# A delta-rule attention and two MoE layers on one core: the first part's order as an explicit list, and the key products in 64x32 tiles

## The chip, the cores and the metric

One core of a Trainium2 chip runs the whole program. The metric is the device time in microseconds (us) of one execution, where lower is better. It is told as the median of several runs.

## The reference

Three layers run one after the other on 4 batches of 768 tokens, 3072 tokens in all, 384 wide.

1. A delta rule with 8 heads of 48. With k normalized, each head keeps a 48x48 state. At every token `y_t = q_t S`, and then `S += beta_t * k_t (v_t - k_t S)`. The tokens of one sequence depend on each other in order.
2. A dense feed-forward layer with 2048 inner columns: `h = x w_in`, `g = h * clip(h + 3, 0, 6) / 6`, `x = g w_out`.
3. A mixture of 8 experts: each token goes to the expert with the largest gate, through `relu(x w1) w2`, weighted by its probability.

All inputs and outputs are float32, and the kernel keeps that accuracy by splitting each operand into a high and a low half and by adding three products (high by high, high by low, low by high).

## The kernel before, in words

**Chunks.** The delta rule is done in 12 chunks of 64 tokens. Two batches lie beside each other on the 128 partitions, so there are 24 iterations `it`: chunk `it // 2`, batch pair `it % 2`. Four iterations make a group `g`, and there are six groups.

**The first part** (up to about 506 us of the span) holds the delta rule and the first 7 of the 16 slices of 128 inner columns of the dense layer. It is written as 31 Python generators, called streams. Each yields one operation at a time, or a list of TensorE products that stay together. The ones that matter here:

- `kl_stream`, `n_stream`, `k_stream`: load k, take its norms (tiles `ksq`, `ss`, `s`, `rn`), and write the normalized k as a high and a low half into `Kbd`. `kt_stream` and `kg_stream` turn it by DMA transposes into `KTb`, `QTb` or `KG`.
- `g_stream` (line 603): the key products `pG`, for each iteration the products of all keys of a chunk with each other. Each of the 8 heads takes 3 products for each of the two 64-partition halves, so 48 products. From them ScalarE copies the diagonal 32x32 blocks into `Dt` (four copies of 32 partitions) and writes the off-diagonal block as two halves `MC`.
- `t_stream` (line 634), `s_stream`, `z_stream`: for each group a VectorE transposition `Bt<-Dt`, a product with beta on GpSimd, a substitution of 31 steps of two VectorE operations (`sub`, `Xp`), a transposition `Bt<-Xp`, the halves `TT`, and the products `pZ` of 32x32 tiles.
- `chain(0)`, `chain(1)`: the recurrence of each batch pair, with products `pR`, `pW` twice and `pS`, each 24 products, and evictions by ScalarE and VectorE between them. `o_stream` makes the output products `pO` (96 products of 64x64 tiles); `p_stream` makes `pP`, `x_stream` the transposes `pX`.
- `m_stream`: the dense layer of a chunk, 84 rounds in all of 9 products `ph`, the activation (ScalarE `t`, VectorE `t`, ScalarE `gH`, GpSimd `gL`) and 6 products `py`. `wi_stream` and `wo_stream` prepare its weights; four VectorE operations on `nws` narrow each slice.
- `ahead_stream`: the first three slices of the weights for the second part.

**What sets the order.** `drive` (line 1078) runs the streams while the program is built. `Clock` (line 39) holds a planner's costs of each operation; `drive` takes the operation that could start first by these costs and breaks near ties by the table of due times `DUE`. `pin` (line 164) then ties each operation to the one before it on its engine, so each engine's order is fixed in the program. On the chip an engine takes its operations in that order, each as soon as its inputs are there. The loads and the DMA transposes are issued by SyncE, also in the order in which they were planned.

**The second part** is the rest of the dense layer (lines 1410 to 1480), then the routing and the experts. No line of it is touched.

Of the kernel before, what the change touches and what calls it, by code (L numbers as in the profile page):

```python
# [38 lines left out]
class Clock:  # L39


    def __init__(self, tc):
        self.tc, self.last = tc, {}
        self.free = dict(pe=0.0, act=0.0, dve=600.0, pool=3100.0, dma=0.0)
        self.columns = {}
        self.written, self.read, self.bus, self.issue = {}, {}, 0.0, 0.0
        self.slot, self.count, self.parts = {}, {}, {}
        self.runs, self.phase, self.tick, self.warm = [], 0.0, 0, False
        self.mode = 128, False
        self.place, self.end = {}, dict(act=0.0, dve=0.0)  # L50

    def tile(self, pool, shape, dt, tag, bufs, name):
        t = pool.tile(shape, dt, tag=tag, name=name, bufs=bufs)
        n = self.count[tag] = self.count.get(tag, -1) + 1
        self.slot[t.name] = (tag, n % bufs)
        return t

    def keys(self, ap):

        n = ap.name  # L60
        if n in self.parts:
            return [(n, x) for x in self.parts[n](ap)]
        return [self.slot.get(n, n)]

    def cost(self, op):

        n = 1
        for d in (op.ins[0] if "reduce" in op.fn.__name__ else op.out).shape[1:]:
            n *= d
        if "dma" in op.fn.__name__:  # L70
            return 40
        half = (op.ins[-1] if op.eng == "pe" else op.out).dtype in (FP16, FP32R, BF16)
        if op.eng == "pe":
            if op.ins[-1].dtype == FP32R:
                return n / 2.2
            if op.ins[-1].shape[0] <= 64:
                return max(32 if op.ins[-1].shape[0] == 64 else 25.2, n / 2.4) / op.tiles
            return max(25.5, n / 2.4 + 2.5) if half else 0.85 * max(n, 128)
        fn = op.fn.__name__
        pointers = sum(x.free_size() == 1 for x in op.ins[1:])  # L80
        if op.eng == "act":
            return (52 if op.ins[0].space == PSUM else 109) + 95 * (pointers > 0) + 84 * (len(op.outs) > 1) + 0.836 * n
        if op.eng == "dve":
            if half and fn == "tensor_copy":
                return 64 + 0.26 * n
            if fn == "memset":
                return 60 + (0.38 if half else 0.82) * n
            if fn == "transpose":
                return 70 + 1.06 * n
            if fn == "reciprocal":  # L90
                return 70 + 6 * n
            if fn == "tensor_scalar" and op.ins[0].space != PSUM:
                return 66 + 0.52 * n + 60 * (pointers > 0)
            return 70 + (0.52 if all(x.dtype == FP16 for x in op.ins) else 1.04) * n + 60 * (pointers > 0)
        if op.eng == "pool":
            if fn in ("memset", "tensor_copy"):
                return 80 + 0.81 * n
            wide = op.out.dtype == FP32R or op.out.shape[-1] == 32
            return 60 + (2.5 if wide else 2.15) * n
        raise ValueError(op.eng)  # L100

    def places(self, op):

        r, w = {}, (op.out.space, op.out.start_partition())
        for x in op.ins:
            r.setdefault(x.space, x.start_partition())
        return r, w

    def held(self, op):

        r, w = self.places(op)
        now = self.place.setdefault(op.eng, ({}, {}))
        return any(now[0].get(m, x) != x for m, x in r.items()) or now[1].get(w[0], w[1]) != w[1]

    def shared(self, op):

        if op.eng != "dve" or op.fn.__name__ in ("memset", "transpose", "tensor_reduce", "reciprocal"):
            return False
        wide = [x for x in op.ins if x.free_size() > 1]
        sb = [x for x in wide if x.space != PSUM]  # L120
        if op.fn.__name__ in ("tensor_copy", "tensor_scalar"):
            return bool(sb) and op.out.space != PSUM
        return len(sb) > 1

    def unshared(self, t):

        for a, b in reversed(self.runs):
            if b < t:
                break
            if a <= t:  # L130
                return b
        return t

    def matmul(self, op, t):

        n, tick = op.out.free_size(), int((t + self.phase) * 3 / 10240)
        rows = op.ins[-1].shape[0]
        half = op.ins[-1].dtype in (FP16, FP32R, BF16)
        while self.tick < tick:
            self.warm = self.columns.get(self.tick, 0.0) >= (3060 if self.warm else 3350)  # L140
            self.tick += 1
        self.columns[tick] = self.columns.get(tick, 0.0) + n * (1 if half else 2) * rows / 128
        mode, last = (32 if rows <= 32 else 64 if rows <= 64 else 128, op.ins[-1].dtype == FP32R), self.mode
        self.mode = mode
        turn = 90 * (mode[0] != last[0]) + (0 if mode[1] == last[1] else 85 if mode[1] else 13)
        if self.warm:
            return turn + self.cost(op)
        if rows <= 64:
            return turn + max(53.4 if rows == 64 else 42, n / 1.2) / op.tiles
        return turn + (max(27, n / 1.2) if half else 1.7 * max(n, 128))  # L150

    def ready(self, tiles):
        return max([self.free["pe"]] + [self.written.get(k, 0.0) for x in tiles for k in self.keys(x)])

    def start(self, ops):
        t = 0.0
        for op in ops:
            t = max([t] + [self.read.get(k, 0.0) for x in op.outs for k in self.keys(x)] + [self.written.get(k, 0.0) for x in op.ins for k in self.keys(x)])
        t = max(self.free[ops[0].eng], t + {"pe": 54, "pool": 77}.get(ops[0].eng, 33))
        if ops[0].eng in self.end and "dma" not in ops[0].fn.__name__ and self.held(ops[0]):  # L160
            t = max(t, self.end[ops[0].eng] + 13)
        return self.unshared(t) if self.shared(ops[0]) else t
# [9 lines left out]
    def emit(self, ops):  # L172
        t = t0 = self.start(ops)
        for op in ops:
            t += self.cost(op) if op.eng != "pe" else self.matmul(op, t)
            self.pin(op)
        self.free[ops[0].eng] = t
        if "dma" in ops[0].fn.__name__:
            o = ops[0].out
            n = 2 if o.dtype == FP16 else 4  # L180
            turn = "transpose" in ops[0].fn.__name__
            rate = 200 if turn else 170 if n * o.shape[-1] < 512 else 320
            for d in o.shape:
                n *= d
            self.issue = max(self.issue, t) + 600
            self.bus = max(self.bus, self.issue + 650) + n / rate
            if turn:
                self.free["dma"] = self.bus - 870
            elif ops[0].eng == "dma":
                self.free["dma"] = self.issue  # L190
            t = self.bus + 1900
        else:
            if ops[0].eng == "pool":
                if self.runs and t0 - self.runs[-1][1] < 60:
                    self.runs[-1][1] = t + 55
                else:
                    self.runs.append([t0, t + 55])
            t += {"pe": 165, "dve": 84, "act": 95, "pool": 45}[ops[0].eng]
            if ops[0].eng in self.end:
                r, w = self.places(ops[0])  # L200
                now = self.place.setdefault(ops[0].eng, ({}, {}))
                now[0].update(r)
                now[1][w[0]] = w[1]
                self.end[ops[0].eng] = t
        for op in ops:
            for now, used in ((self.written, op.outs), (self.read, op.ins)):
                for k in [k for x in used for k in self.keys(x)]:
                    now[k] = max(now.get(k, 0.0), t)
# [13 lines left out]
def kernel(ctx: ExitStack, tc: tile.TileContext, q, k, v, beta, w_in, w_out, w_gate, w1, w2, out):  # L222
# [137 lines left out]
    with ExitStack() as ax:  # L360
# [717 lines left out]
        def drive(streams):  # L1078
# [6 lines left out]
            def step(x):  # L1085
                while True:
# [4 lines left out]
                    if x[0] != "next":  # L1091
                        break
# [537 lines left out]
```

## Time and profile before

| what | us |
|---|---|
| median of 3 runs | 999.73 |
| lowest and highest | 997.82, 1004.11 |
| the profiled execution: its time | 1003.64 |
| the profiled execution: its span | 1001.9 |
| TensorE matmul busy in the span | 885.3 |
| VectorE, ScalarE, GpSimd busy | 586.2, 569.0, 433.2 |
| TensorE's mean granted clock | 0.983 |

The profile is that of one execution. Its span runs from the first to the last instruction, and its own time is 1.7 us longer. PE is the matmul side of TensorE, PEld its weight loads, DVE is VectorE, ACT ScalarE, POOL GpSimd, SP SyncE. Most operations of the first part are issued from one line, L36, so they are told apart by the names of their tiles. "Issue" as a releaser means that the engine waited for nothing that the profile shows.

### The profile page before, as it was taken

The numbers are of one execution on the slowest core, as the hardware profiler recorded it, in microseconds if no ns is written. First come the engines' busy times: TensorE is split into PE (matmuls) and PEld (weight loads), VectorE is DVE, ScalarE is ACT, GpSimd is POOL, SyncE is SP. The second block draws the span as 40 slices with busy tenths as digits, with TensorE's granted clock in tenths as the row PEclk, the third lists the DMA queues.
The fourth block names the chain that finished last, engine by engine and source line by source line (L and its number), as shares of the span: only waits on it lengthen the run. The fifth ranks groups of instructions, "written<-read, shape, count | busy, mean of one in ns | idle before, by whom it ended". The sixth has DMA issues, their size and how long they took to land.

```text
span 1001.9 us, 27659 instructions
## 1 busy us (share of the span) xinstructions
PE 885.3 (88%) x11454; PEld 819.2 (82%) x11454; DVE 586.2 (59%) x1611; ACT 569.0 (57%) x1195; POOL 433.2 (43%) x446
## 2 busy tenths in 40 slices
PE   1423898889988899999989999999999999999997
PEld 1412888889888798888878899898899999999996
DVE  7888997888979789653487545554534211222221
ACT  4757889779888876755557333323334542455521
POOL 5255565455546524423343204223104936755761
PEclk9999799999999989999999999999999999999999
DMA  7978797996998956566365432332116734434500
GB/s 127 190 145 158 126 179 135 176 139 124 211 198 110 200 112 123 125 155 208 118 218 172 131 93 97 128 96 97 53 61 240 228 105 153 147 114 141 172 21 20
DMA packets 255080, 138.89 MB, mean 139 GB/s; under 512 B 199587, under 2 KB 239845, under 8 KB 254944
## 3 DMA queue, kind: packets, MB, share of 16 engines
q1 hardware_dynamic: 247120, 118.82, 53.5%
q0 software_dynamic: 7280, 17.41, 5.2%
q8 instruction: 91, 1.49, 0.6%
q10 hardware_dynamic: 544, 0.80, 0.2%
q14 instruction: 45, 0.37, 0.1%
HBM read 71.56 MB, written 35.50 MB: 107 GB/s over the span
## 4 chain that ended last, share of the span: by engine, by line
PE 61%; DVE 14%; ACT 8%; issue 7%; DMA 6%; POOL 4%; SPq 0%; POOLq 0%; ACTq 0%
PE ph L1459 11%; PE ph L1250 9%; PE py L36 5%; PE ph L36 5%; PE py L1475 3%; PE py L1474 3%; PE py L1473 3%; PE pz L1238 3%; PE pz L1240 3%; PE pz L1239 3%; DMA KG<-Kbd 2%; DVE Xp L36 2%; DVE sub L36 2%; PE pO L36 2%; PE pW L36 2%
## 5 line engine op out<-in xcount | busy, mean ns | idle before, releaser
L1254 DVE SCALAR_TENSOR_TENSOR hL<-ph,hH 128x384 fp32r<-128x384 f32 (+6 forms) x64 | 36.1, 564 | 163.6 <-ACT hH L1253 163.6
L36 POOL TENSOR_TENSOR gL<-t,gH 128x256 fp32r<-128x256 f32 x84 | 64.6, 769 | 130.8 <-ACT gH L36 122.6
L1253 ACT ACTIVATE hH<-ph 128x384 fp32r<-128x384 f32 (+6 forms) x64 | 31.6, 494 | 104.8 <-PE ph L1250 104.8
L1462 ACT ACTIVATE t<-ph,half 128x512 f32<-128x512 f32 x54 | 37.1, 687 | 76.4 <-PE ph L1459 75.2
L36 PE MATMUL ph<-xTH,wiH 128*128 128x256 f32 x252 | 76.4, 303 | 4.3 <-DVE t L36 3.4
L1419 POOL DMA_INDIRECT slots<-row,di x24 | 23.9, 997 | 125.1 <-DVE di L1411 119.7
L1463 DVE SCALAR_TENSOR_TENSOR t<-t,ph 128x512 f32<-128x512 f32 x54 | 37.1, 686 | 62.8 <-ACT t L1462 62.5
L1238 PE MATMUL pz<-a2H,hH 128*128 128x384 f32 (+1 forms) x216 | 73.2, 339 | 0.4 <-ACT hH L1253 0.4
L36 PE MATMUL ph<-xTL,wiH 128*128 128x256 f32 x252 | 72.2, 286 | 0.7 <-DVE xTL L36 0.7
L1240 PE MATMUL pz<-a2H,hL 128*128 128x384 f32 (+1 forms) x216 | 72.4, 335 | 0.0
L1239 PE MATMUL pz<-a2L,hH 128*128 128x384 f32 (+1 forms) x216 | 72.4, 335 | 0.0
L36 PE MATMUL ph<-xTH,wiL 128*128 128x256 f32 x252 | 71.6, 284 | 0.0
L1271 POOL DMA_INDIRECT out_dram<-yo,rw x29 | 28.0, 967 | 100.7 <-ACT yo L1270 96.5
L1467 DVE TENSOR_TENSOR gL<-t,gH 128x512 fp32r<-128x512 f32 x54 | 47.5, 882 | 32.6 <-ACT gH L1466 32.5
L36 DVE TENSOR_TENSOR Xp<-Xp,sub 128x31 f32<-128x31 f32 (+15 forms) x186 | 64.0, 344 | 2.8
L36 PE MATMUL py<-woH,gH 128*128 128x392 f32 x168 | 64.9, 386 | 0.7 <-issue 0.7
L36 DVE TENSOR_TENSOR sub<-Bt,Xp 128x31 f32<-128x31 f32 (+15 forms) x186 | 61.6, 331 | 2.2
L298 POOL TENSOR_TENSOR a2L<-r,a2H 128x384 fp32r<-128x384 f32 x64 | 62.5, 1009 | 0.0
L36 ACT ACTIVATE t<-ph,half 128x256 f32<-128x256 f32 x84 | 39.6, 471 | 38.4 <-PE ph L36 31.4
L298 POOL TENSOR_TENSOR a1L<-r,a1H 128x512 fp32r<-128x512 f32 x48 | 60.4, 1305 | 0.1
L36 PE MATMUL py<-woH,gL 128*128 128x392 f32 x168 | 58.7, 350 | 0.7 <-POOL gL L36 0.6
L36 DVE SCALAR_TENSOR_TENSOR t<-t,ph 128x256 f32<-128x256 f32 x84 | 35.0, 417 | 40.3 <-ACT t L36 39.3
(318 smaller groups left out, 3141.9 us busy)
## 6 DMA issues: line engine op xcount, KB each, us to landing
r<-in_moe_w_dram SPq DMA_DIRECT2D x32, 768.0 KB, 4.6
slots<-zrow SPq DMA_DIRECT2D x8, 784.0 KB, 6.2
stage<-in_moe_w_in_dram SPq DMA_DIRECT2D x16, 384.0 KB, 3.9
stage<-in_moe_w_out_dram SPq DMA_DIRECT2D x16, 384.0 KB, 3.2
row<-ypart SPq DMA_DIRECT2D x6, 784.0 KB, 4.5
ysave<-row SPq DMA_DIRECT2D x6, 784.0 KB, 3.9
rw<-slots SPq DMA_DIRECT2D x24, 196.0 KB, 3.1
kr<-in_k_dram SPq DMA_DIRECT2D x24, 192.0 KB, 4.6
```

Of the source, the lines that this page charges most:

```text
L36: return self.fn(*self.a, **self.k)
L298: in_order(pool.tensor_tensor(dst[1], src_ap, dst[0].bitcast(FP32), ALU.subtract))
L1238: pe.matmul(o, hh[:, ts_], a2[0][:, fp], start=fp == 0, stop=False)
L1239: pe.matmul(o, hh[:, ts_], a2[1][:, fp], start=False, stop=False)
L1240: pe.matmul(o, hl[:, ts_], a2[0][:, fp], start=False, stop=fp == KF2 - 1)
L1250: pe.matmul(ph, a1[a][:, c, fs], xt[x][:, c, 0:n], start=k == 0, stop=k == 3 * KD - 1)
L1253: act.activation(hH, ph, ACTF.Relu)
L1254: dve.scalar_tensor_tensor(hL, ph, 0.0, hH.bitcast(FP32), ALU.max, ALU.subtract)
L1459: pe.matmul(ph, wi(a, f)[:, c], xt[x][:, c], start=n == 0, stop=n == 3 * KD - 1)
L1462: act.activation(t_, ph, ACTF.Relu, bias=half, scale=1.0 / 6.0)
L1463: dve.scalar_tensor_tensor(t_, t_, 1.0, ph, ALU.min, ALU.mult)
L1467: dve.tensor_tensor(gL, t_, gH.bitcast(FP32), ALU.subtract)
```

## The change

Four things change, all in the first part.

1. The planner goes. `Clock` becomes `Order`, which keeps only `tile`, `pin` and `emit`, and `DUE` becomes `ORDER`, a string of 2926 letters, one for each operation (or list of products) of the first part. A letter names the stream whose next operation is issued. The order of all engines and of the DMA queue thus comes from the string.
2. In `g_stream` the 64x64 products become 64x32 ones: for each head, each of the three halves' products and each of the two partition halves, the two groups of 32 output partitions are written by a product of their own. That makes 96 products for an iteration in place of 48. The first group's product streams its own 32 keys twice, so columns 32 to 63 of `pG` then hold the diagonal block on all 128 partitions, and one ScalarE copy takes the place of four.
3. In `n_stream` the squares of the first group alternate between the tiles `ksq` and `vsq`.
4. In `t_stream` the product with beta of the first group is done by VectorE, the others still by GpSimd.

```diff
-class Clock:
+class Order:
...
     def emit(self, ops):
-        t = t0 = self.start(ops)
         for op in ops:
-            t += self.cost(op) if op.eng != "pe" else self.matmul(op, t)
             self.pin(op)
...
-            yield "take", lambda: clk.ready(inputs) if freeb else None
+            yield "take", lambda: freeb or None
...
-                    sq_ = tmp([128, H, D], FP32, "ksq", 1)
+                    sq_ = tmp([128, H, D], FP32, "ksq" if g or j % 2 else "vsq")
...
-                yield [o for u in range(H) for o in halves(lambda r: (p_[r, u], [kt[r, x, u, r] for x in range(2)], [kt[r, x, u, r] for x in range(2)]), True, True)]
+                ops = []
+                for u in range(H):
+                    for n, (a, b) in enumerate(((0, 0), (0, 1), (1, 0))):
+                        for blk in range(2):
+                            for bb in range(2):
+                                k = slice(64 * bb, 64 * bb + 64)
+                                r = slice(64 * bb + 32 * blk, 64 * bb + 32 * blk + 32)
+                                x = kt[k, b, u, k] if blk else kt[k, b, u, r].unsqueeze(1).to_broadcast([64, 2, 32])
+                                o = p_[r, u] if blk else p_[r, u].rearrange("p (x t) -> p x t", x=2)
+                                ops.append(PE.matmul(o, kt[k, a, u, r], x, start=n == 0, stop=n == 2))
+                                ops[-1].tiles = 4
+                yield ops
...
-                for x in range(4):
-                    r = slice(32 * x, 32 * x + 32)
-                    c = slice(32 * (x % 2), 32 * (x % 2) + 32)
-                    yield ACT.activation(Dt[r, :, 8 * j:8 * j + 8], p_[r, :, c].rearrange("p u i -> p i u"), ACTF.Copy)
+                yield ACT.activation(Dt[:, :, 8 * j:8 * j + 8], p_[:, :, 32:64].rearrange("p u i -> p i u"), ACTF.Copy)
...
-                yield POOL.tensor_tensor(Bt, Bt, bY[:, g].unsqueeze(1).to_broadcast([128, 32, 32]), ALU.mult)
+                yield (POOL if g else DVE).tensor_tensor(Bt, Bt, bY[:, g].unsqueeze(1).to_broadcast([128, 32, 32]), ALU.mult)
...
+            for n in [ALPHABET.index(c) for c in "".join(ORDER)]:
+                if isinstance(now[n], tuple):
+                    assert now[n][0] == "take" and now[n][1]() is not None, (n, now[n])
+                    step(n)
+                assert isinstance(now[n], list), (n, now[n])
+                clk.emit(now[n])
+                step(n)
+                settle()
...
+        ALPHABET = "0123456789abcdefghijklmnopqrstu"
+        ORDER = [
+            "kskrkakakskjssjrsaarrsssjrrssbbbrbbprspbbbbsbbbbbbbqqqrrqnrqsnrnnjnsqnjnpopnonsqdsroqnsmnqqrsnnnsqsr",
...
```

The letters are the streams in the order of the call of `drive`: 0 and 1 the two chains, 4 and 5 `o_stream`, c and d the transposes of k, f `p_stream`, i `z_stream`, l `s_stream`, m `g_stream`, r and s the weights, t `m_stream`, u `ahead_stream`.

## Rows read from the trace of the kernel before

**Rows 1.** The page, parts 1 and 2: busy us; tenths in 40 slices.
```profile
PE 885.3 (88%) x11454; PEld 819.2 (82%) x11454; DVE 586.2 (59%) x1611; ACT 569.0 (57%) x1195; POOL 433.2 (43%) x446
...
PE   1423898889988899999989999999999999999997
```
**Rows 2.** Busy time by stretch: us, PE, PEld, DVE, ACT, POOL, PEclk, DMA share, GB/s.
```profile
0.00:100.00 100.00, 28.32 (x557) 24.57 (x557) 81.38 (x250) 60.61 (x135) 48.92 (x53) 1.00 0.85 155
100.00:505.00 405.00, 371.08 (x8177) 345.28 (x8177) 312.46 (x909) 310.49 (x669) 184.48 (x185) 0.97 0.79 152
100.00:350.00 250.00, 224.34 (x5460) 210.61 (x5462) 215.71 (x653) 212.90 (x460) 131.89 (x128) 0.97 0.94 160
```
**Rows 3.** PE's waits, 100:505: waited for, us in total, times, longest us.
```profile
PE pW L36 <- DVE W L36: 4.1, 1, 4.1
PE ph L36 <- DVE t L36: 3.4, 5, 1.4
...
PE pW L36 <- issue: 1.8, 1, 1.8
...
PE pP L36 <- issue: 1.3, 1, 1.3
...
PE pO L36 <- issue: 0.9, 1, 0.9
...
PE py L36 <- issue: 0.7, 1, 0.7
```
**Rows 4.** Timeline of DVE, 49:89: start us, us, operation.
```profile
49.70 1.24 DVE L36 STREAM_TRANSPOSE Bt<-Dt 128x1024 f32<-128x1024 f32 x1
...
53.57 0.18 DVE L36 TENSOR_TENSOR sub<-Bt,Xp 128x31 f32<-128x31 f32 x1
...
87.10 1.25 DVE L36 STREAM_TRANSPOSE Bt<-Xp 128x1024 f32<-128x1024 f32 x1
```
**Rows 5.** Lines of DVE, 0:49.7: xcount, busy us, mean ns, idle before.
```profile
L36 DVE SCALAR_TENSOR_TENSOR nws<-stage,nws 128x384 int32<-128x384 int32 x14 | 7.6, 544 | 0.2
...
L36 DVE TENSOR_SCALAR nws<-nws 128x384 f32<-128x384 f32 (+1 forms) x14 | 4.9, 351 | 0.3 <-ACT nws L36 0.3
L36 DVE CAST W<-idq 32x256 f16<-32x256 f32 x8 | 3.1, 389 | 0.1
```
**Rows 6.** Timeline of POOL, 50:54, the first product with beta.
```profile
51.19 2.35 POOL L36 TENSOR_TENSOR Bt<-Bt,bY 128x1024 f32<-128x1024 f32 x1
```
**Rows 7.** Timeline of ACT, 7:12.5, the first squares.
```profile
8.88 0.52 ACT L36 ACTIVATE ksq<-kr 128x384 f32<-128x384 f32 x1 [0.62 <-DVE padb L1433]
...
11.34 0.52 ACT L36 ACTIVATE ksq<-kr 128x384 f32<-128x384 f32 x1 [0.62 <-DVE ss L36]
```
**Rows 8.** Lines of ACT, 0:505, the copies of the diagonal.
```profile
L36 ACT ACTIVATE Dt<-pG 32x256 f32<-32x256 f32 x96 | 35.8, 373 | 4.7 <-PE pG L36 3.4
```
**Rows 9.** Waits of DVE, 100:505, the longest two.
```profile
DVE t L36 <- ACT t L36: 39.3, 32, 2.5
DVE uL L36 <- ACT uH L36: 15.0, 12, 2.5
```
**Rows 10.** Timeline of PE: groups of small products, 33:42, 121:124, 144:146, 177:180.
```profile
34.18 2.77 PE L36 MATMUL pG<-KTb 64*64 64x64 f16 x96
...
122.15 1.49 PE L36 MATMUL pG<-KG 64*64 64x64 f16 x48
...
144.37 0.94 PE L36 MATMUL pG<-KG 64*64 64x64 f16 x48
...
177.32 0.76 PE L36 MATMUL pZ<-TT,MC 32*32 32x32 f16 x48
```
**Rows 11.** The chain that ended last, 190:193: start us, us, what.
```profile
191.15 1.63 PE pO L36 x96
```
**Rows 12.** Timeline of PE, 192:196.5, within one group of 24 products.
```profile
195.82 0.18 PE L36 MATMUL pW<-uL,W 128*128 128x48 f16 x1 [1.85 <-issue]
```
**Rows 13.** The page, part 3: PE's program: packets, MB, share.
```profile
q8 instruction: 91, 1.49, 0.6%
```

More of the change, by code (lines that the diff above doesn't have):

```diff
@@ L36, in now @@
         return self.fn(*self.a, **self.k)
-class Clock:
+class Order:
     def __init__(self, tc):
         self.tc, self.last = tc, {}
[L44 to L50, printed above, removed]
-    def tile(self, pool, shape, dt, tag, bufs, name):
[L53 to L162, printed above, removed]
@@ L164, in pin @@
+    def tile(self, pool, shape, dt, tag, bufs, name):
+        return pool.tile(shape, dt, tag=tag, name=name, bufs=bufs)
     def pin(self, op):
@@ L172, in emit @@
     def emit(self, ops):
-        t = t0 = self.start(ops)
         for op in ops:
-            t += self.cost(op) if op.eng != "pe" else self.matmul(op, t)
             self.pin(op)
[L177 to L208, printed above, removed]
 class Defer:
@@ L395, in read @@
                 return self.pr
-        clk = Clock(tc)
+        clk = Order(tc)
         def ring(name, n, cols=128):
@@ L1024 @@
         phb = psA.tile([128, 2, 256], FP32, tag="ph", name="ph", bufs=1)
-        clk.parts[phb.name] = lambda ap: [ap.offset // 256]
         nph = [0]
@@ L1078, in drive, with step @@
         def drive(streams):
-            st = []
-            for n, (gen, due) in enumerate(zip(streams, DUE)):
-                due = [float(x) for x in due.split()]
-                st.append([None, due, n, gen, due.pop(0)])
-            def step(x):
+            now = [None] * len(streams)
+            def step(n):
+                now[n] = "next"
+                while now[n] == "next":
+                    now[n] = next(streams[n], None)
+                if now[n] is not None and not isinstance(now[n], (tuple, list)):
+                    now[n] = [now[n]]
@@ L1086, in step, with settle @@
+            def settle():
                 while True:
-                    x[0] = next(x[3], None)
-                    if x[0] is None:
-                        st.remove(x)
+                    go = [n for n, x in enumerate(now) if isinstance(x, tuple) and x[0] == "need" and x[1]()]
+                    if not go:
                         return
-                    if x[0] != "next":
-                        break
-                    x[4] = x[1].pop(0) if x[1] else x[4]
-                if not isinstance(x[0], (tuple, list)):
-                    x[0] = [x[0]]
@@ L1097, in start @@
-            def start(x):
-                y = x[0]
-                if isinstance(y, tuple):
-                    ok = y[1]()
-                    return ok if y[0] == "take" and ok is not None else -1.0 if ok else None
-                return clk.start(y)
-            for x in list(st):
-                step(x)
-            while st:
-                ready = [(start(x), x[2], x) for x in st]
-                ready = [x for x in ready if x[0] is not None]
-                assert ready, [x[3].__name__ for x in st]
-                t, _, x = min(ready, key=lambda y: y[:2])
-                if isinstance(x[0], list):
-                    eng = x[0][0].eng
-                    end = t + TOL * sum(clk.cost(o) for o in x[0])
-                    same = [y for y in ready if isinstance(y[2][0], list) and y[2][0][0].eng == eng and y[0] <= end]
-                    t, _, x = min(same, key=lambda y: (y[2][4], y[0]))
-                    clk.emit(x[0])
-                step(x)
@@ L1120 @@
-        TOL = 0.041028
-        DUE = [
[31 rows of a table removed]
+                    for n in go:
+                        step(n)
+            for n in range(len(streams)):
+                step(n)
[3 more added lines that the diff above has]
+                    assert now[n][0] == "take" and now[n][1]() is not None, (n, now[n])
+                    step(n)
+                assert isinstance(now[n], list), (n, now[n])
+                clk.emit(now[n])
+                step(n)
+                settle()
```

31 lines of the change are left out of this document (30 added, 1 removed), and 31 rows, old and new, of the table DUE.

## The prediction

> **What bounds the kernel now.** I read the busy shares and slices first, then the stretch that the change touches, then who makes TensorE wait there. Over the span PE is busy 88%, and only its first four slices of 25 us are low [rows 1]. The first part falls in two [rows 2]. Up to 100 us PE is busy 28.3 of 100 us and VectorE 81.4: a chain through VectorE must end before the recurrence can begin. From 100 to 505 us PE is busy 371.1 of 405 us, which leaves 33.9 us idle. That idle time is split among many waits: the longest is a single 4.1 us, the next sums to 3.4 us over five, and four waits on nothing that the profile shows ("issue") sum to 1.8 + 1.3 + 0.9 + 0.7 = 4.7 us [rows 3]. So three sums matter: the time to 100 us, the 33.9 us of holes after it, and PE's own work. A busy PE is not yet a PE at its peak, so shorter work is possible in principle, but nothing in the change shortens PE's products.
>
> **The startup.** In the new list I counted what stands ahead of the first `Bt<-Dt` on VectorE. There are 24 narrowing operations where the trace has 28, and 3 identity copies where it has 8 [rows 5]. Four narrowing operations at (7.6 + 4.9) / 28 = 0.45 us are 1.8 us. Five copies at 0.39 us are 1.9 us. The product with beta took 2.35 us on GpSimd [rows 6]. On VectorE I take the 1.24 us of the transposition of the same 128x1024 [rows 4], so 1.1 us less latency, but VectorE did other work beneath GpSimd's 2.35 us, so this may come to nothing. Two squares waited 0.62 us each for the one buffer to be read [rows 7]; the second tile takes this wait away, about 1.2 us on the way to the norms. The three diagonal copies saved per iteration are 3 x 0.373 = 1.1 us of ScalarE [rows 8] just ahead of the transposition. Between the two transpositions (49.7 to 87.1 us [rows 4]) the list holds the same substitution with weights and norms between its steps, which I take as equal. The sum could be 1.8 + 1.9 + 1.2 + 1.1 + 1.1 = 7.1 us; some of it overlaps. I take **-5 us**, bounds -7 and 0 (the DMA transposes could end last instead).
>
> **The copies.** 72 of 96 diagonal copies go; the 24 left cover 128 partitions by 256, at about the same 0.373 us each [rows 8]. That takes 72 x 0.373 = 26.9 us from ScalarE, about a sixteenth of its first part. ScalarE is busy 212.9 of 250 us between 100 and 350 us, and VectorE waits 39.3 us for ScalarE's `t` and 15.0 us for `uH` [rows 2, 9]; VectorE's results are what PE waits for most [rows 3]. So a lighter ScalarE shortens PE's waits indirectly. VectorE itself, 215.7 of 250 us [rows 2], gets no lighter, so it is late next.
>
> **The order.** Of the 33.9 us of holes, 33.9 - 4.7 = 29.2 us are waits for data. The list moves operations singly where the planner had 31 tables of due times. What it places is the same work: in the list the 22nd `pS` comes after 66 of the 84 dense rounds and the last `pW` after 74, so the recurrence still reaches almost to the end and dense rounds fill its gaps. No row prices a new order. From both sides it is -29 (all data waits gone) and +29 (as many again, if the list puts late operands first). I take half the waits gone, **-14 us**, as ScalarE's load falls where the longest waits pass through it; this is a judgement, and its error is the widest one.
>
> **The key products.** 24 groups of 48 products become 24 of 96. A group of 48 took 1.49 us at 122 us and 0.94 us at 144 us [rows 10]; I take the later one. Sixteen groups come after 100 us, on PE's path; the earlier eight lie beneath the startup chain. If four 64x32 tiles run side by side as two 64x64 ones did, 96 products take 0.94 us again: 0 us. The nearest rows for 96 products are `pO`, 1.63 us [rows 11], and `pZ`, 0.76 us for 48, so 1.52 us for 96 [rows 10]. At 1.63 us the cost is 16 x 0.69 = 11 us. I take 1.2 us, between these, as the tiles are smaller than those of `pO` and four in number: 16 x 0.26, **+4 us**. Less than nothing is excluded, since each group streams the same columns. The Trainium skill speaks for the lower end here: TensorE: Matmul & The Clock Gate, section "Part 3: Packing small matmuls", says that products on different tiles overlap, with about 4 ns of issue each. By that this term would be 0 and the total 4 us lower; no run here shows four tiles of this shape.
>
> **TensorE's program.** PE's program arrives in packets: 91 of them, 1.49 MB [rows 13], for 11454 products with a weight load each [rows 1], so about 126 products to a packet. A wait with nothing to wait for, 1.85 us, stands inside a group of 24 equal products [rows 12]. It follows 96 `pO` that began at 191.15 us [rows 11], 24 `pS` and 19 `pW`: 139 products in 195.82 - 191.15 = 4.67 us, wait included. I read this as a piece of the program that was not there yet, with a turn of about 4.5 us for a piece. The new program has 1152 more products, 9 more pieces, with hardly more work. A mean product after 100 us takes 371.1 / 8177 = 45 ns [rows 2]. A piece that holds a whole new group does 0.94 us for 96 products and 30 x 0.045 = 1.4 us for the rest, 2.3 us, so it may wait 4.5 - 2.3 = 2.2 us. In the list 11 of the 16 groups after 100 us stand next to the long `ph` or `py`, 5 do not: 5 x 2.2 = 11 us, of which I take half, since data waits cover some: **+5 us**. Bounds 0 and 16 x 2.2 = 35 us. A rule of the Trainium skill speaks against any such cost: Runtime: NRT & Kernel Launch, section "Instruction fetch mechanics", says that crossing a block of the program is mostly hidden. The trace does not agree at 1.85 us; by the rule this term would be 0.
>
> **The sum.** -5 - 14 + 4 + 5 = -10 us. The profiled execution took 1003.64 us, its span 1001.9; the median is 999.73, 3.9 us below. A difference carries over: 1003.6 - 10 = 993.6 for such an execution, and 999.7 - 10 = 989.7, **990 us**, for the median. That is 1.0% less, right where a measurement of this kernel (about 1%) begins to tell it from no change. All of the second part is untouched and hides nothing of this, since PE is the bound there too.
>
> **The rivals.**
> - *The waits return behind VectorE.* It is busy 86% from 100 to 350 us and not relieved [rows 2], so PE's holes only move. Then -5 + 0 + 4 + 5 = +4: 1004 us, no change that can be told. For it speaks that the recurrence keeps its place in the list; against it ScalarE's 26.9 us. Chance 0.25.
> - *TensorE's program ends on the other side.* At every new group the piece is late: +35 in place of +5, 20 more than the gains of 5 + 14 less 4 can pay. The sum is -5 - 14 + 4 + 35 = +20: 1020 us. It decides above 15 us (no gain is left), and is told from no change above 25 us. For it speaks the 1.85 us inside a group [rows 12]; against it that all such waits sum to 4.7 us now [rows 3]. Chance 0.12.
> - *Nearly all holes fill.* -7 - 25 + 4 + 0 = -28: 972 us. For it speaks that of PE's waits shown only one lasts over 2 us, so none is a hard bound [rows 3]; against it that VectorE stays loaded. Chance 0.13.
> - *Program delivery costs nothing more.* The pieces arrive beneath other waits, so -5 - 14 + 4 + 0 = -15: 985 us. For it speaks that three of the four waits are 1.3 us or less [rows 3]; against it the short pieces above. This is what the rule on instruction fetch would make of it. Chance 0.08.
>
> **How the numbers follow.** The forecast has 0.42; its own range is 980 to 998 us. It lies on the 1% bound (989.7 us), so I give 0.25 of it to faster, 0.16 to no change, 0.01 to slower. Faster is then 0.25 + 0.13 + 0.08 = 0.46. No change is 0.16 + 0.24 + 0.01 = 0.41, slower 0.01 + 0.01 + 0.11 = 0.13. The range of 8 in 10 goes from 973 to 1006 us: it leaves out half of the case at 972 and nearly all of that at 1020, takes in the case at 1004 with the 2 us that runs differ, and takes in the ends of the key products (0 and +11).
>
> **What would show it.** The startup: `Bt<-Xp` of the first group at 82 us, not 87.1, and PE's work in 0:100 above 28.3 us. The copies: `Dt` x24, 9 us in place of 35.8. The key products: the time of a `pG` group of 96 after 144 us, 0.94 to 1.63 us. The program: the issue waits of PE above 4.7 us, near 10, at groups that follow `pG` or `pO`. The order: idle PE between the first `pW` and the end of the first part under 33.9 us, near 25 with the issue waits in it. I am wrong if the first part ends later than at 506 us, or if the second part (496 us of the span) changes by more than 3 us.

## The result: slower by 0.65%, where 1% faster was forecast

The changed kernel takes 1007.39 us (median), beside 1001.81 us for the kernel before in the same rounds: a ratio of 1.0065, with a 95% interval of 1.0045 to 1.0086. The forecast was 990 us, the range 973 to 1006 us. The profiled execution of after took 1008.00 us (span 1006.1 us), near its median, so its rows can be read beside those of before (1003.64 us, span 1001.9 us).

The page of after, parts 1 to 3, against [rows 1, 13]:

```profile
PE 891.2 (89%) x12606; PEld 823.8 (82%) x12606; DVE 587.7 (58%) x1612; ACT 540.0 (54%) x1123; POOL 429.1 (43%) x445
...
PE   1427888889888999989998999999999999999997
...
q8 instruction: 100, 1.64, 0.7%
```

ScalarE is 29 us lighter (569.0 before), as 72 fewer copies would have it, and PE's program is 9 packets longer; VectorE is not lighter. Windows of after (us, PE, PEld, DVE, ACT, POOL, PEclk, DMA share, GB/s): the first two answer to [rows 2], the last three are cut at the first `pW` and at the first product of the second part. Behind them is the same cut of before:

```profile
0.00:100.00 100.00, 37.30 (x1170) 32.87 (x1171) 91.52 (x267) 56.78 (x124) 48.88 (x53) 1.00 0.98 168
100.00:505.00 405.00, 365.20 (x8696) 339.65 (x8695) 301.66 (x886) 281.94 (x601) 178.66 (x182) 0.95 0.74 148
...
0.00:86.64 86.64, 26.20 (x797) 22.52 (x798) 78.60 (x227) 47.26 (x104) 43.59 (x49) 1.00 0.94 163
86.64:513.41 426.77, 382.45 (x9100) 354.63 (x9100) 322.37 (x950) 296.18 (x632) 187.24 (x194) 0.95 0.75 150
513.41:1006.10 492.69, 482.53 (x2710) 446.66 (x2710) 186.69 (x437) 196.54 (x388) 198.29 (x204) 1.00 0.38 124
```

```profile
0.00:100.17 100.17, 28.32 (x558) 24.58 (x558) 81.55 (x251) 60.78 (x135) 48.92 (x53) 1.00 0.85 155
100.17:507.59 407.42, 372.66 (x8188) 346.73 (x8188) 314.88 (x921) 311.87 (x672) 185.79 (x187) 0.97 0.79 152
507.59:1001.90 494.31, 484.37 (x2710) 447.84 (x2710) 189.78 (x441) 196.40 (x389) 198.46 (x206) 0.99 0.39 125
```

These rows account for the whole change of the span. Up to the first `pW` PE idles 60.4 us in place of 71.9: -11.4. From there to the second part it idles 44.3 us in place of 34.8: +9.6. Its busy time in the first part is 26.2 + 382.5 = 408.7 us in place of 401.0: +7.7, at a lower mean clock. That is +5.8 at the start of the second part (513.4 against 507.6 us), and the untouched second part gives back 1.6.

What fills the 44.3 us is another kind of wait. PE's waits in after, 86.64:513.41 (us in total, times, longest), against [rows 3]:

```profile
PE ph L36 <- DVE t L36: 12.4, 16, 1.6
PE pP L36 <- issue: 7.4, 3, 3.0
PE pG L36 <- issue: 4.9, 4, 1.6
PE pO L36 <- issue: 4.9, 3, 2.3
PE pZ L36 <- issue: 3.2, 2, 2.1
PE pW L36 <- issue: 2.1, 2, 1.5
PE pS L36 <- issue: 1.4, 2, 1.2
...
PE pR L36 <- issue: 0.2, 1, 0.2
```

The issue rows sum to 24.1 us in 17 waits (4.7 in 4 before). The waits for VectorE's `t` went from 3.4 to 12.4 us, and all other waits for data from 25.0 to 6.5 us (each without the wait that the first `pW` itself ends, 4.1 us before and 0.2 after, which lies ahead of the stretch). So the waits for data fell from 28.4 to 18.9 us, 9.5 us, and more than that came back as issue waits. That the fall is not the list's work alone is shown by e1 below. One issue wait in the chain of after (start us, us, what):

```profile
246.14 0.88 PE pG L36 x96
247.02 0.48 PE pX L36 x3
247.50 0.90 PE pO L36 x50
248.40 2.34 issue
250.74 1.36 PE pO L36 x46
```

It lies inside one group of 96 products that wait for nothing that the profile shows. Ahead of it are 149 products in 2.3 us: the new `pG`, three transposes and half a `pO`. What PE waits for there is its own program, and the places of the waits show it. Between the ends of the waits at 214.82 and 250.74 us PE issued 767 products and 768 weight loads, between those at 403.01 and 453.08 us 896 and 895: six and seven times 256 instructions, to within one (windows of after, columns as above):

```profile
214.82:250.72 35.90, 32.96 (x767) 30.95 (x768) 31.15 (x108) 27.60 (x58) 16.12 (x18) 0.90 0.80 146
403.01:453.06 50.05, 44.14 (x896) 41.32 (x895) 26.91 (x65) 29.26 (x65) 15.33 (x17) 0.92 0.57 139
```

So it is with all 17 waits, and with all 141 issue waits of PE in this stretch of the fourteen kernels timed here: they end at one and the same place in a count of 256 of PE's instructions, to within one, and each 1.2 to 1.8 us after a packet of the instruction queue has landed. The packet of the wait above landed at 249.54 us (queues of after, 248.3:249.6):

```profile
q8 instruction: 1, 0.02, 5.6%
```

A packet is thus 256 instructions, 128 products with a weight load each. Of the 71 packets that came in this stretch, 17 came late.

The clock falls behind the wait shown (windows of after):

```profile
240.00:250.70 10.70, 8.24 (x231) 7.54 (x227) 10.41 (x30) 8.47 (x16) 5.74 (x7) 1.00 1.20 211
250.70:254.30 3.60, 3.56 (x53) 3.50 (x53) 1.64 (x5) 2.09 (x4) 0.00 (x0) 0.53 1.33 164
254.30:262.00 7.70, 6.14 (x164) 5.62 (x162) 5.86 (x20) 5.19 (x12) 2.44 (x2) 1.00 0.54 131
```

The granted clock is 2.4 GHz up to the wait and 0.53 of it, hence nearly all at 1.2 GHz, in the 3.6 us that follow it, while PE is busy nearly all the time. The products behind this wait are slow as well.

### The profile page after: what moved, and what is told of

It reads as the page before. It is cut to its first block, busy times and chain, and to the rows that moved or that the text cites. A ratio compares the mean times of both kernels' runs of the same rounds, so it can differ in the third digit from the quotient of the medians.

```text
span 1006.1 us, 29868 instructions
## 1 busy us (share of the span) xinstructions
PE 891.2 (89%) x12606; PEld 823.8 (82%) x12606; DVE 587.7 (58%) x1612; ACT 540.0 (54%) x1123; POOL 429.1 (43%) x445
## 4 chain that ended last, share of the span: by engine, by line
PE 69%; DVE 15%; issue 7%; ACT 4%; POOL 3%; POOLq 0%; ACTq 0%; DVEq 0%
PE ph L1304 11%; PE ph L1095 8%; PE ph L36 8%; PE py L36 8%; PE py L1320 3%; PE py L1319 3%; PE py L1318 3%; PE pO L36 3%; PE pz L1083 3%; PE pz L1085 3%; PE pz L1084 3%; PE pW L36 2%; DVE sub L36 2%; DVE Xp L36 2%; DVE nws L36 2%
## 5 line engine op out<-in xcount | busy, mean ns | idle before, releaser
L36 PE MATMUL ph<-xTH,wiH 128*128 128x256 f32 x252 | 77.5, 307 | 12.6 <-DVE t L36 12.4
L36 PEld LDWEIGHTS ph<-xTH,wiH 128*128 128x128 f32 x252 | 48.9, 194 | 21.7 <-DVE t L36 21.5
L36 ACT ACTIVATE t<-ph,half 128x256 f32<-128x256 f32 x84 | 39.7, 473 | 47.4 <-PE ph L36 40.7
L148 POOL TENSOR_TENSOR a1L<-r,a1H 128x512 fp32r<-128x512 f32 x48 | 60.4, 1298 | 0.1
```

The lines of the kernel that those rows point to most:

```text
L36: return self.fn(*self.a, **self.k)
L148: in_order(pool.tensor_tensor(dst[1], src_ap, dst[0].bitcast(FP32), ALU.subtract))
```

## The experiments

Each was timed in five rounds beside the kernel before, in three sets. Idle and issue are PE's, from the first `pW` to the second part; the last three columns are of one profiled execution each, which need not be a typical one: that of e1 (1003.41 us) was the longest of its 12, those of e3 (1000.00), e6 (995.40) and e4 (1005.84) were the shortest or next to it.

| kernel | median us | ratio to before [95%] | first `pW` us | idle | issue |
|---|---|---|---|---|---|
| before (in the rounds of after) | 1001.81 | | 100.2 | 34.8 | 4.7 |
| after | 1007.39 | 1.0065 [1.0045, 1.0086] | 86.6 | 44.3 | 24.1 |
| e0_oldlist | 1001.12 | 0.9992 [0.9971, 1.0012] | 100.7 | 33.0 | 4.6 |
| e1_neworder_oldG | 999.66 | 0.9975 [0.9952, 0.9998] | 88.7 | 40.7 | 9.4 |
| e2_oldorder_newG | 1012.39 | 1.0112 [1.0083, 1.0142] | 101.0 | 42.1 | 13.3 |
| e3_split | 1004.56 | 1.0030 [1.0004, 1.0056] | 86.7 | 37.7 | 14.7 |
| e4_start | 1010.15 | 1.0076 [1.0048, 1.0105] | 88.9 | 46.3 | 5.3 |
| e5_half | 1004.05 | 1.0019 [0.9996, 1.0042] | 88.7 | 45.1 | 6.7 |
| e6_mended | 998.48 | 0.9974 [0.9948, 1.0000] | 88.7 | 39.9 | 4.7 |
| e7_columns | 1024.55 | 1.0217 [1.0179, 1.0255] | 103.8 | 37.4 | 7.3 |
| e8_oldstart | 1007.94 | 1.0074 [1.0046, 1.0102] | 102.5 | 40.5 | 8.0 |
| e9_copies | 1012.45 | 1.0111 [1.0072, 1.0151] | 88.7 | 46.8 | 20.1 |
| e10_oldparts | 1006.98 | 1.0063 [1.0039, 1.0087] | 87.5 | 47.0 | 27.9 |
| e11_order | 1001.71 | 1.0006 [0.9988, 1.0025] | 88.7 | 39.0 | 6.2 |

### Order and key products, each alone

**e0_oldlist**: the planner's order written out as a list, everything else as before.

> The planner's own order of the kernel before, written down as a list of 2998 letters and replayed, with the 64x64 key products, four diagonal copies, one tile for the squares and the product with beta on GpSimd as before. Only which of three PSUM banks a product takes may differ. Every theory expects the time of the kernel before, within 0.3%, and its 4.7 us of issue waits on PE between the first pW and the dense layer's second part; if it is slower, the bank choice is part of the story.

**e1_neworder_oldG**: after, with the key products and copies of before.

```diff
-                                 ops.append(PE.matmul(o, kt[k, a, u, r], x, start=n == 0, stop=n == 2))
-                                 ops[-1].tiles = 4
-                yield ops
+                yield [o for u in range(H) for o in halves(...)]
...
-                yield ACT.activation(Dt[:, :, 8 * j:8 * j + 8], p_[:, :, 32:64]..., ACTF.Copy)
+                yield [four copies of 32 partitions]
```

> The new list with the 48 products of 64x64 tiles and four diagonal copies (issued as one letter) in place of 96 products and one copy. Program theory (1152 more products make pieces of TensorE's program come late): issue waits on PE after the first pW fall from 23.5 us to under 10 us, the first pW stays near 87 us, the time falls to 985 to 993 us although ScalarE gets 27 us back. Order theory (the list itself puts short products too close): issue waits stay above 15 us and the time above 1000 us. Copies theory (a lighter ScalarE is what the list gains by): DVE and ACT waits of PE grow by 10 us or more.

**e2_oldorder_newG**: the planner's order as a list, with the key products and the one copy of after.

> The old order as a list, with the 96 products of 64x32 tiles and one diagonal copy for each iteration; squares and product with beta as before. Program theory: issue waits on PE rise from 4.7 us to 12 us or more, and the time to 1005 to 1012 us. Order theory: issue waits stay under 8 us and the time at 995 to 1001 us, as ScalarE has 27 us less.

The list as a form changes nothing that can be told (e0). The four kernels make a square: the new key products cost 1012.39 - 1001.12 = 11.3 us in the old order and 1007.39 - 999.66 = 7.7 us in the new one (by the ratios 12.0 and 9.0 us); the new order gains 1.5 us with the old key products, which is within the intervals, and 5.0 us with the new. So the loss is the key products', as the program theory said, and their issue waits came out as it expected in e1 and e2. But e1 missed its 985 to 993 us: its recurrence starts 12 us earlier and the end gains hardly anything. Windows of e1, then of e0, up to the first `pW` and from there to the second part:

```profile
0.00:88.71 88.71, 26.50 (x461) 22.94 (x462) 77.50 (x227) 54.63 (x124) 43.84 (x49) 1.00 0.89 164
88.71:509.29 420.58, 379.85 (x8284) 350.71 (x8284) 319.67 (x950) 316.59 (x684) 186.85 (x194) 0.96 0.73 151
```

```profile
0.00:100.67 100.67, 28.33 (x557) 24.60 (x557) 81.47 (x251) 60.76 (x135) 48.91 (x53) 1.00 0.83 154
100.67:505.66 404.99, 372.02 (x8188) 345.96 (x8188) 314.01 (x921) 312.14 (x672) 185.94 (x187) 0.97 0.79 152
```

In this execution of e1 PE idles 10.1 us less ahead of the first `pW` and 7.7 us more behind it, and it is busy 6.0 us more for the same products. Behind the first `pW` its waits for data are 30.2 us, and e0's 27.0: the list alone does not fill the holes for data. From e1 to after they fall to 18.9 us while the issue waits grow from 9.4 to 24.1: what PE loses to its program there, it no longer waits for data, in large part. This is also what the copies theory of e1 expected (waits for data longer by 10 us or more with the old copies), so the two are told apart only by e9 below. In the old order the program's waits came on top: 27.0 us of waits for data in e0, 27.1 in e2.

In e2 a key group takes what it took before, so its 11.3 us are not PE's work: its PE is busy 400.3 us in the first part, e0's 400.3. Its issue waits are 13.3 us in place of 4.6, and six of them fall in the `pO` groups (waits of e2):

```profile
PE pO L36 <- issue: 6.6, 6, 2.5
...
PE pP L36 <- issue: 3.1, 3, 1.3
```

### What makes the program late: its length or its pace

**e7_columns**: old order, the key products 96 of 64x64 tiles over 32 columns each, so as many instructions as the change has, on two tiles.

```diff
-                yield [o for u in range(H) for o in halves(...)]
+                for c in range(2):
+                    for n, (a, b) in enumerate(((0, 0), (0, 1), (1, 0))):
+                        for bb in range(2):
+                            ops.append(PE.matmul(p_[r, u, 32 * c:32 * c + 32], kt[r, a, u, r], kt[r, b, u, k], ...))
```

> The order of the kernel before as a list, old squares and old product with beta, four diagonal copies in a row; the key products are 96 of 64x64 tiles over 32 columns each in place of 48 over 64 columns: as many instructions as the change has, but on two tiles of the old form. If the number of PE's instructions is the price (program theory): 100 packets on the instruction queue, issue waits near 13 us, 1008 to 1015 us, as with the 64x32 tiles in the old order. If the 64x32 form on four tiles is the price, 1000 to 1003 us and issue waits near 5 us.

**e3_split**: after, with 7 `pG` groups and 13 `pO` groups issued in two halves and a `ph` or `py` between them. One place, by what PE issues (the number is the iteration):

```diff
- pP11 pO11(96) py pZ
+ pP11 pO11(48) py pO11(48) pZ
```

> The changed kernel with 7 of its groups of 96 key products and 13 of its groups of 96 output products each cut in two halves of 48 with one or two groups of the dense layer's products between them; the rest of the order stays. If late pieces come from runs of short products (density), issue waits fall from 23.5 us to 12 to 17 us and the time by 6 us or more against the changed kernel. If each piece costs a fixed wait, or the waits come from elsewhere, both stay within 2 us, and the added switches of tile size cost up to 3 us.

e7 came out at 1024.55 us, which neither theory gave. Its 96 products do not run abreast as those of after do (timeline of e7, then of after):

```profile
140.71 1.69 PE L36 MATMUL pG<-KG 64*64 64x32 f16 x96
```

```profile
129.31 0.95 PE L36 MATMUL pG<-KG 64*32 64x64 f16 x96
```

So e7 pays in PE's work: 423.3 us busy in the first part, 23 more than e0. But it has the same 100 packets of program as e2 and after, and its issue waits are 7.3 us, not 13.3. The number of instructions is not the price by itself; the price comes where they pass in half the time, so that a packet of 256 is used up before the next has landed. That agrees with e3: the same instructions as after with long products in between have 14.7 us of issue waits in place of 24.1, as density would have it. But the time, 1004.56 us in place of 1007.39, falls by less than the 6 us expected, the two intervals overlap, and the waits are those of its fastest execution. It is busy 407.7 us, only 1.0 less than after, though its clock is back at 0.97 from 0.95 between 100 and 505 us. The further changes from one kind of group to another may take up what the clock returns; no run shows it.

### Where the earlier start went

**e4_start**: the new list up to its first `pW`, the old order behind it; old key products. **e5_half**: the new list up to the 22nd dense round. **e8_oldstart**: the reverse of e4. For all three the edit is in the list alone:

```diff
-        ORDER = [new list]
+        ORDER = [one list up to the cut, then the other list without the letters already used]
```

> The list of after up to and with its first pW, behind it the order of the kernel before for all that is left; the key products as before (48 of 64x64), the squares' second tile and the product with beta as after. Theory A (the list behind the start gives the startup back: PE's waits for DVE t, its dense runs, the lower clock after each): first pW near 88 us, PE's waits for DVE t back near 4 us, issue waits near 5 us, second part starts near 496 us, 990 to 993 us. Theory B (an earlier start only lengthens the holes behind it, because the first part is bounded by PE's work and the recurrence's chain, whatever the order): second part starts near 505 us, 999 to 1001 us, as with the whole list.

> As the kernel with only the start of the list, but the list of after holds up to its 22nd dense round (near 200 us), the old order behind it. If the list gives its start back evenly along its length (theory A), a value between: 993 to 997 us, second part near 500 us. If the loss sits at the two waits inside pP near 397 and 449 us and the rounds behind them, as with the start alone: 990 to 993 us. Theory B: 999 to 1001 us.

> The order of the kernel before up to and with its first pW, behind it the list of after for all that is left; old key products, new squares and product with beta. It completes the square of start and rest: old start and old rest gave 0.9992, new and new 0.9975, new start and old rest 1.0076 of the time before. Theory A (the rest of the list is better in itself, the start is worth nothing): first pW near 100 us, ratio 0.995 to 1.000. Theory B (a rest is worth something only behind the start that it was made for): ratio 1.005 to 1.012, as with new start and old rest.

Old start and old rest have a ratio of 0.9992, new and new 0.9975, but new and old 1.0076 and old and new 1.0074. So theory A of e4 is wrong: the rest of the list does not give the start back, since the old rest does worse behind the same start. Its theory B (999 to 1001 us) missed too, and e5, with half of the list, lies between at 1004.05 us, outside all that was expected of it; only e8 came out as one of its theories had it, its B. A new start by itself gains nothing, and neither does a new rest. In e4 the lead is gone early: its first `Bt<-Xp` starts at 81.20 us (e0: 87.61), its second at 147.99 (147.72), so the second group's substitution on VectorE has already used it up. In after the lead lasts longer, and the timelines show it going: the first `pW` of after comes 13.5 us earlier than before's, but the ninth group of state products (`pS`) is only 2.7 us earlier (before, then after; the first product of each group):

```profile
100.17 0.22 PE L36 MATMUL pW<-uH,W 128*128 128x48 f16 x1 [4.08 <-DVE W L36]
...
233.52 0.20 PE L36 MATMUL pS<-uH,Kbd 128*128 128x48 f16 x1
```

```profile
86.64 0.22 PE L36 MATMUL pW<-uH,W 128*128 128x48 f16 x1 [0.23 <-DVE W L36]
...
230.83 0.18 PE L36 MATMUL pS<-uH,Kbd 128*128 128x48 f16 x1
```

In e1, without the new key products, it is 230.68 us. From 100 to 505 us PE is busy nine tenths of the time (365.2 of 405 us in after), and the recurrence shares it with the dense rounds. Idle time ahead of the first `pW` was exchanged for idle time behind it (e4: 62.4 + 46.3 = 108.7 us idle in the first part; e0: 72.3 + 33.0 = 105.3). These 3.4 us are less than half of what e4 loses to e0 (8.4 us by the ratios); its profiled execution was 4.3 us under its median, and where the rest goes is not shown.

### Moving the waits about

**e6_mended**: e1 with letters moved at seven places: away from the dense runs ahead of two long issue waits, and to put work between the first two dense rounds of a step. One place (`ph8.1` is round 1 of dense chunk 8):

```diff
- pX17 pW19 pO18 pP19 pW19 ph8.0 ph8.1
+ pX17 pW19 ph8.0 pO18 pP19 pW19 ph8.1
```

> The whole list with the old key products, but letters moved at seven places: first ph of three steps ahead of pG, pS, pO groups that stood before it, second ph of three steps behind pW, pP groups that stood after it, one pO behind the py after it. Nothing is added or removed. If dense runs and the second ph of a step are what the list loses by, issue waits fall from 9.3 to 4 to 6 us, the waits for DVE t from 18.4 to 13 to 15 us, the low clock behind the two long pP waits goes, and the time is 990 to 995 us. If the places do not matter (theory B), 999 to 1001 us.

**e11_order**: e6 with more letters moved at the 20 places where PE waited for `t`. One place:

```diff
- ph6.3 py6.2 ph6.4 pP16
+ ph6.3 py6.2 pP16 ph6.4
```

> The list with moved letters (e6_mended), with more letters moved at the 20 places where PE waited 16.0 us in all for DVE t there: ScalarE's t earlier past the ScalarE operations that stood between it and its ph, or one PE group of the recurrence pulled ahead of the next ph. If those waits are lost time: they fall to 6 to 9 us and the time to 990 to 995 us. If the hole moves to other waits: 997 to 1000 us, as e6_mended (998.5), with the waits for other operands that much longer.

In e1 the chain shows such a run: 115 products (96 `pO` and 19 `pP`) in 2.3 us, behind 24 `pW`, and then the longest but one of its issue waits:

```profile
392.06 0.60 PE pW L36 x24
392.66 1.63 PE pO L36 x96
394.29 0.66 PE pP L36 x19
394.95 2.71 issue
397.66 0.43 PE pP L36 x5
```

In e6 both of e1's long waits in `pP` are gone and the issue waits fall from 9.4 to 4.7 us. The clock is full from end to end of the recurrence (window of e6, 85:500), and PE's busy time in the first part falls from 406.3 to 398.1 us for the same products:

```profile
85.00:500.00 415.00, 372.45 (x8329) 342.36 (x8328) 321.87 (x951) 320.12 (x693) 188.69 (x194) 1.00 0.75 155
```

But this sets one of e6's fastest executions (995 us) beside e1's slowest. The median of e6 is 998.48 us, outside the 990 to 995 expected, and its ratio cannot be told from e1's. e11 is plainer. Its waits for `t` fall as meant (waits of e6, then of e11):

```profile
PE ph L36 <- DVE t L36: 16.0, 20, 1.6
```

```profile
PE ph L36 <- DVE t L36: 5.0, 10, 1.2
```

Its idle time stays at 39.0 us (39.9 in e6), because the other waits for data went from 17.7 to 27.2 us, and it is not faster. The wait for data that was taken away at one place came back at another; here the sum over all waits is what must be looked at.

### ScalarE's relief, and the small parts of the start

**e9_copies**: after with its one diagonal copy made in four pieces again.

```diff
-                yield ACT.activation(Dt[:, :, 8 * j:8 * j + 8], p_[:, :, 32:64]..., ACTF.Copy)
+                yield [ACT.activation(Dt[r, :, 8 * j:8 * j + 8], p_[r, :, 32:64]..., ACTF.Copy) for r in four]
```

> After, with its diagonal copy made in four pieces of 32 partitions again: 72 copies more on ScalarE, some 0.37 us each, 27 us; nothing else changes. If ScalarE's relief shortens the waits of TensorE (a part of my 14 us): after's 1007 plus 4 to 14 us. If ScalarE is not where the waits come from: within 2 us of after.

**e10_oldparts**: after with one tile for the squares and the first product with beta on GpSimd.

```diff
-   sq_ = tmp([128, H, D], FP32, "ksq" if g or j % 2 else "vsq")
+   sq_ = tmp([128, H, D], FP32, "ksq", 1)
-   yield (POOL if g else DVE).tensor_tensor(Bt, Bt, bY[:, g]..., ALU.mult)
+   yield POOL.tensor_tensor(Bt, Bt, bY[:, g]..., ALU.mult)
```

> After, with one tile for the squares again and the first product with beta on GpSimd again. By the startup's terms (1.2 and 1.1 us) the first Bt<-Xp comes 1 to 2.5 us later than 79.4 us. If a later start costs the end as much: 1008 to 1010 us. If the lead at the start is lost in the holes behind it anyway: 1006 to 1008 us, no difference that can be told.

e9's ratio is 0.46% above after's, 4.6 us: the low end of what was expected, and the two intervals overlap a little, so its size is not settled. Its waits for data are 25.2 us, after's 18.9, so the lighter ScalarE goes with 6.3 of the 11.3 us by which e1 has more. e9 also differs from e1 in hardly more than the key products: its ratio is 1.36% higher, 13.6 us, which is what the 96 products cost in the new list without the relief of the copies. e10 brings the first `Bt<-Xp` 0.9 us later (80.30 us; 1 to 2.5 expected) and no difference in time.

## Why the prediction was wrong, by its own steps

Two steps failed, and the larger is **the order**, with the lead of the startup carried to the end: -14 and -5 us. e1 against e0 measures them, the small parts of the start included, with the old key products and copies: 1.5 us by medians, 1.7 by the ratios, within the intervals. With the copies' relief, which the -14 counted in (e9, some 4.6 us), the 19 us become some 6. The lead came, 10.1 us less idle time ahead of the first `pW`. But the waits for data, of which half were to go, are 30.2 us in e1 and 27.0 in e0, and the issue waits and PE's busy time grew. No row priced the new order, as the prediction says itself.

The second is **TensorE's program**. It was seen, and its rival had 0.12, but the term of +5 us was mis-sized. The issue waits grew by 19.4 us in after, 14.7 of them from e1 to after, and by 8.7 us in the old order alone (e2). Two things were wrong in its working. It halved the price because waits for data were to cover some of it: in the old order nothing was covered. In the new order most was, as far as one execution of each shows (from e1 to after 14.7 us more issue waits and 3.6 more idle time), and e1's was its longest. And it let only the key products next to short work wait, 5 of 16 groups; the waits also fall in the `pO`, `pP` and `pZ` groups behind them, 17 waits in all, since a packet is used up over all groups that it holds. "Issue waits near 10 us" was 24.1. The program and the key products together were +9 us; they cost 7.7 us by medians and 9.0 by the ratios, but with the copies' relief in it, which the forecast had elsewhere. Without it they cost 13.6 us (e9 against e1), and since the products themselves cost nothing, this is the price of the program with whatever the clock adds. That 9 came out so near is luck.

PE's busy time apart from the key products was put at nothing, and no term had the **clock**, though the rows of before show 0.97 there. The busy time of the first part grew by 7.7 us, and e1 is already 6.0 us above e0. e6 against e1, the same products at a mean clock of 1.00 and 0.96, gives an estimate: 398.1 and 406.3 us busy, 2 us for each hundredth, so some 4 us of the 7.7 for 0.95 in place of 0.97. Other pairs do not bear it out (e0: 0.97 and 400.3 us, e11: 0.99 and 404.2), so it is not shown. The clock does move with the time from one execution of a kernel to the next: of after's 20 the two at a mean of 0.984 and 0.987 took 1000.32 and 1003.73 us, the two at 0.973 took 1011.46 and 1014.60. That a wait makes the clock fall is suggested, but not shown. Seven of the eight stretches at the lower clock behind after's first `pW` begin within 2 us of the end of an issue wait. But behind the wait of 2.17 us that ends at 162.78 the clock is full, and before's longest stretch at the lower clock lies at 112 to 125 us, ahead of its first issue wait (windows of after, then of before):

```profile
162.78:169.00 6.22, 6.22 (x158) 5.83 (x159) 4.21 (x15) 3.94 (x10) 3.23 (x4) 1.00 0.60 87
```

```profile
111.80:125.00 13.20, 10.98 (x266) 10.31 (x260) 12.84 (x37) 11.29 (x24) 7.94 (x8) 0.50 0.79 114
```

The other terms:

- **The startup**, -5 us with bounds -7 and 0: the first transposition came at 41.80 us (49.70 before), and `Bt<-Xp` at 79.43, below the 82 expected and outside the bounds (7.7 us). The 37.4 us between the two were taken as equal and were 37.6. But that such a lead reaches the end was wrong: e1 and e4.
- **The data waits**, -14 us: 28.4 to 18.9 us, -9.5. That looks nearly right, but it is not what the order did: e1 has 30.2. The row of 4.1 us that the prediction counts among the holes after 100 us lies ahead of them: it ends at 100.17 us. And ScalarE's relief did not act where it was looked for. The 26.9 us are a fourteenth of ScalarE's 371 us there, not a sixteenth, and VectorE's wait for ScalarE's `t` grew from 39.3 us [rows 9] (waits of VectorE in after, 100:505):

```profile
DVE t L36 <- ACT t L36: 46.2, 36, 4.0
```

- **The key products**, +4 us with bounds 0 and +11: 0. A group of 96 took 0.95 us (129.31 us above), that of 48 before 0.94 us [rows 10]. The rule of the Trainium skill (TensorE: Matmul & The Clock Gate, section "Part 3: Packing small matmuls"), that products on different tiles overlap, had it right, and e7 shows the difference the tiles make: 1.69 us on two tiles.
- **The second part** changed by 1.6 us, within the 3 given.

Of the rivals, two hold a part of it: "The waits return behind VectorE" (1004 us) that the holes only move, as in e1, and "TensorE's program ends on the other side" the late program, though its 35 us were more than twice the 13.6, and it kept the gains of 5 and 14. The other rule of the Trainium skill that was weighed, that the crossing of a block of the program is mostly hidden (Runtime: NRT & Kernel Launch, "Instruction fetch mechanics"), is borne out at 54 of 71 packets, which show no wait on issue, but not in the price: the 17 waits are 24.1 us.

Open is how the 7.7 to 9.0 us of the key products divide between the waits themselves and slow products, what lowers the clock, and why a rest of a list is worth 8 to 10 us less behind another start. The best order measured is that of e1, with the old key products: 0.9975 [0.9952, 0.9998] of the time before; e6 is its equal, and neither can be told from e0 (0.9992).

## What to carry to other kernels

Where a change makes more and shorter instructions for an engine, look in the chain for waits on "issue" inside a group of equal products, and price the new instructions by how fast they pass, together with the dense groups behind them: 96 products at 10 ns each left 13.3 us of waits, at 18 ns each 7.3 us. Count the instructions too: here PE's program came in packets of 256, and every wait on issue fell between two of them. Waits for data may hide a late program (in the new order much of it, in the old order nothing), so the two must not be priced apart. A lead at the start is a gain only if the order behind it can use it: try it with the rest that is to follow.

## Seen and not expected

In none of the 83 pairs of dense rounds did a `ph` begin before VectorE's `t` of the round just before had ended, in before, e1 and after alike, though the program gives successive rounds two halves of one tile. So `ph` waits for `t` whenever less work lies between than `t` takes on ScalarE (0.47 us) and VectorE (0.42 us) with the handoffs. What makes it wait, the program's own semaphores or something else, is not shown, and two tiles were not tried.
